# Another order of the opening steps in a packed attention and feed-forward kernel

## The chip, the cores and the metric

The kernel runs on one core of one Trainium2 chip. The metric is the device time of one execution in microseconds (us). Before the change it is 703.89 us, the median of three runs (703.79 to 703.93). The engines are named as the profile names them: PE is the matrix engine (PEld its weight loads), DVE the vector engine, ACT the scalar engine, POOL the GpSimd engine, and SP the engine that issues nearly all DMAs.

## The reference

There are 8 batches of 8 heads, 576 tokens and 64 columns a head. For each head, 32 packing queries `p` attend to the keys and values, and the 576 queries then attend to the 32 packed rows, which serve as keys and values both. The heads are laid side by side (512 columns), and a feed-forward layer of 2048 hidden columns follows.

```python
def sm_attn(qq, kk, vv):
    s = scale * np.matmul(qq, kk.transpose(0, 1, 3, 2))
    a = np.exp(s - np.max(s, axis=-1, keepdims=True))
    a = a / (np.sum(a, axis=-1, keepdims=True) + 1e-09)
    return np.matmul(a, vv)
p_packed = sm_attn(p, k, v)
x = sm_attn(q, p_packed, p_packed)      # tokens x 512
h = x @ w_in                            # 512 x 2048
out = (h * (1.0 / (1.0 + np.exp(-h)))) @ w_out
```

## The kernel before

**The work.** The kernel never builds `x`. It multiplies the packed rows of a batch by `w_in` (a "pack", `pp`, line 250) and the second attention's shares by that product (`h`, line 563), so the hidden values of a batch come from 32 shares a head. A unit is one block of 128 hidden columns of one batch: `h` makes its products, `g` applies the activation (ACT, lines 582 to 588), `l` takes the rounding rest (DVE, line 593), and `o` multiplies by `w_out` and adds up in PSUM (line 603). From the fifth unit on, each product is made of three products of a faster 32-bit type (a high part and a low part of each operand); the first four units (`WHOLE`) use plain float32.

**The weights.** `w_in` and `w_out` arrive as 64-bit numbers in 20 chunks. A chunk is fetched (`wf`, SP, line 191), scaled and rounded on ACT (`ws`, `wr`, lines 197 and 201), bounded, signed and shifted on DVE (`wz`, `wg`, `wt`, lines 205, 209, 216), and joined (`wj`, line 220) on POOL if its number is in `ON_POOL`, else on DVE. Chunks of `w_out` are then split into two parts (`wu` on ACT, line 236; `wl` on DVE, line 240).

**The attention of one batch** is written as steps with a letter each. Those that matter here: `as` scores of the packing queries (PE, line 250, tile `kvq_t`), `ac` their copy to SBUF (ACT, line 276), `am`, `ax` largest value and exponential (DVE 286, ACT 296), `at`, `ay` turning by products with the identity and copying back (PE 315, ACT or DVE 333), `aa` packed rows (PE 348), `an`, `ai`, `aj` scaling, turning and copying them (DVE 358, PE 367, ACT 371, tile `ppT`). Then the second attention, in two halves of the tokens (`.0` and `.1`): `aS` scores (PE 250), `aC` copy (ACT 392), `aB` turning (PE 400), `aM`, `aE` largest and its subtraction (DVE 430, 441), `aX` exponential (ACT 450), `aD`, `aG` sums and shares (DVE 459 to 475), `aU` turning back (PE 420, 423), `aF` copy of the shares (ACT 486), after which `h` may begin.

**The order.** For the first two batches and the weights, nothing is scheduled by a tool: the table `ORDER` (line 54) is read from left to right, and each word is one step; the instructions of a step go to the end of the queues of their engines, in that order, PE, DVE, ACT and SP alike. Each engine works its queue strictly in order, so a waiting instruction holds up all behind it on its engine. The later batches follow a loop with fixed places.

**Filler.** `W` followed by a number is `keep_warm` (line 139): so many products of the identity with itself, whose result nobody reads. One costs two instructions in the trace. The filler's tile comes from `ps_two`, the pool of two PSUM buffers that `as`, `pp` and `h` use as well, so filler may have to wait for a buffer.

**Loads.** Keys, values and queries take turns in a pool of two buffers (`kvq_t`); the queries of batch 0 go to other tiles (`o` and `rest`). Loads and weight chunks share one SP queue.

## Time and profile before

| | |
|---|---|
| median of three runs | 703.89 us |
| the profiled execution's own time | 703.09 us |
| its span, first to last instruction | 701.3 us |
| PE busy | 693.3 us (99%), 5058 matmul instructions |
| DVE, ACT busy | 326.2 us (47%), 331.0 us (47%) |
| POOL busy | 28.7 us (4%) |
| DMA moved | 64.61 MB |

How to read it: the profiled execution spends 1.8 us outside the span of its instructions. PE is busy nearly all the time, so the time can only move where PE waits or does work that isn't needed; the shares of DVE and ACT are averages over the whole span, and in the first 80 us both are far busier than that. In the rows of the time line the first number is the start, the second the length, both in us; `x8` at a row's end is a count of instructions, and brackets name the idle time before them and what ended it.

### The profile page before, as it was taken

The page shows a single profiled execution, that of the slowest core. Times are in us where ns is not written, and L with a number is a line of the kernel's source. Part 1 is how long each engine was busy: PE and PEld are TensorE (multiplying, and loading weights), DVE is VectorE, ACT ScalarE, POOL GpSimd, SP SyncE. Part 2 cuts the span into 40 slices and gives each one's busy share as a digit, 9 for nine tenths or more (in the row PEclk, how much of TensorE's full clock was granted, in tenths as well). Part 3 has the DMA queues.
Part 4 walks back from the last instruction along what each step waited for, and adds up shares of the span by engine and source line. Part 5 has one row for each costly group of instructions (what it writes and reads, how often), then busy time and mean ns, then how long its engine had stood idle before and what let it go on. Part 6 is the DMA issues. An engine that isn't in the chain of part 4 may idle for free.

```text
span 701.3 us, 12059 instructions
## 1 busy us (share of the span) xinstructions
PE 693.3 (99%) x5058; PEld 560.5 (80%) x5058; DVE 326.2 (47%) x482; ACT 331.0 (47%) x614; POOL 28.7 (4%) x19
## 2 busy tenths in 40 slices
PE   8999999999999999999999999999999999999997
PEld 5557788878787888888788888878878788788886
DVE  4999948764534136333532335342372323622111
ACT  4997866637245244451633526452442533433221
POOL 1041022110000000000000000000000000000000
PEclk9999999999999999999999999999999999999999
DMA  9775333634221320313012131123202120010002
GB/s 358 288 304 206 134 121 114 193 141 156 70 81 69 77 104 1 128 33 137 12 61 84 27 107 49 61 72 70 110 0 76 68 36 1 1 60 1 1 1 75
DMA packets 28309, 64.61 MB, mean 92 GB/s; under 512 B 16736, under 2 KB 16736, under 8 KB 23904
## 3 DMA queue, kind: packets, MB, share of 16 engines
q1 hardware_dynamic: 28160, 63.71, 26.2%
q8 instruction: 40, 0.66, 0.4%
q10 hardware_dynamic: 96, 0.13, 0.1%
q14 instruction: 13, 0.11, 0.0%
HBM read 48.76 MB, written 11.53 MB: 86 GB/s over the span
## 4 chain that ended last, share of the span: by engine, by line
PE 97%; ACT 1%; DMA 1%; DVE 1%; issue 0%; ACTq 0%; DVEq 0%
PE ps_acc L603 58%; PE ps_two L563 29%; PE ps_two L250 7%; PE ps_two L348 2%; DMA kvq_t<-in_pkT 1%; PE ps_acc L250 0%; ACT tm L296 0%; PE ps_two L144 0%; ACT tm L392 0%; ACT w_raw L201 0%; ACT win L201 0%; PE ps_two L315 0%; PE ps_two L367 0%; PE ps_acc L315 0%; DVE mx L286 0%
## 5 line engine op out<-in xcount | busy, mean ns | idle before, releaser
L603 PE MATMUL ps_acc<-wo_hi,g_hi 128*128 128x512 f32 x560 | 223.8, 400 | 0.0
L603 PE MATMUL ps_acc<-wo_hi,g_lo 128*128 128x512 f32 x560 | 219.4, 392 | 0.0
L603 PE MATMUL ps_acc<-wo_lo,g_hi 128*128 128x512 f32 x560 | 218.8, 391 | 0.0
L593 DVE TENSOR_TENSOR g_lo<-g,g_hi 128x512 fp32r<-128x512 f32 x124 | 88.9, 717 | 259.5 <-ACT g_hi L584 259.5
L582 ACT ACTIVATE g<-ps_two 128x512 f32<-128x512 f32 x124 | 74.1, 598 | 263.9 <-PE ps_two L563 239.9
L563 PE MATMUL ps_two<-a_lo,pw_hi 128*128 128x288 f32 (+2 forms) x528 | 154.6, 301 | 0.1
L563 PE MATMUL ps_two<-a_hi,pw_hi 128*128 128x288 f32 (+1 forms) x496 | 146.5, 295 | 0.0
L563 PE MATMUL ps_two<-a_hi,pw_lo 128*128 128x288 f32 (+1 forms) x496 | 145.9, 294 | 0.0
L603 PEld LDWEIGHTS ps_acc<-wo_hi,g_hi 128*128 128x128 f32 x560 | 105.1, 188 | 39.3 <-issue 19.9
L603 PEld LDWEIGHTS ps_acc<-wo_hi,g_lo 128*128 128x128 f32 x560 | 105.1, 188 | 24.5 <-DVE g_lo L593 0.4
L603 PEld LDWEIGHTS ps_acc<-wo_lo,g_hi 128*128 128x128 f32 x560 | 105.2, 188 | 18.4
L563 PEld LDWEIGHTS ps_two<-a_lo,pw_hi 128*128 128x128 f32 x528 | 99.1, 188 | 6.2 <-issue 1.4
L563 PEld LDWEIGHTS ps_two<-a_hi,pw_hi 128*128 128x128 f32 x496 | 93.1, 188 | 4.5 <-issue 0.8
L563 PEld LDWEIGHTS ps_two<-a_hi,pw_lo 128*128 128x128 f32 x496 | 93.2, 188 | 0.0
L584 ACT ACTIVATE g_hi<-ps_two 128x512 fp32r<-128x512 f32 x124 | 73.6, 593 | 10.9 <-PE ps_acc L603 10.9
L531 DVE TENSOR_TENSOR pw_lo<-ps_two,pw_hi 128x1024 fp32r<-128x1024 f32 x31 | 36.8, 1219 | 12.8 <-ACT pw_hi L528 12.8
L528 ACT CAST pw_hi<-ps_two 128x1024 fp32r<-128x1024 f32 x31 | 30.2, 1015 | 20.9 <-PE ps_two L250 20.9
L250 PE MATMUL ps_two<-win,ppT 64*32 64x512 f32 (+1 forms) x560 | 32.8, 560 | 0.4 <-POOL win L220 0.4
L586 ACT ACTIVATE rest<-ps_two 128x64 f32<-128x64 f32 x112 | 25.9, 231 | 0.0
L582 ACT ACT_TABLE_LOAD x16 | 20.5, 1283 | 1.5 <-PE ps_two L563 1.0
L250 PEld LDWEIGHTS ps_two<-win,ppT 64*32 64x32 f32 x560 | 7.9, 105 | 14.5 <-issue 11.1
L573 ACT CAST g_hi<-rest 128x512 fp32r<-128x512 f32 x16 | 9.9, 624 | 13.5 <-PE ps_acc L603 13.2
(122 smaller groups left out, 485.0 us busy)
## 6 DMA issues: line engine op xcount, KB each, us to landing
kvq_t<-in_v SPq DMA_DIRECT2D x8, 1280.0 KB, 6.1
kvq_t<-in_pkT SPq DMA_DIRECT2D x7, 1216.0 KB, 6.6
out<-o SPq DMA_DIRECT2D x16, 512.0 KB, 2.8
kvq_t<-in_qT SPq DMA_DIRECT2D x7, 1152.0 KB, 6.5
w_raw<-in_w_in SPq DMA_DIRECT2D x6, 1024.0 KB, 7.5
win<-in_w_out SPq DMA_DIRECT2D x3, 1024.0 KB, 4.5
w_raw<-in_w_out SPq DMA_DIRECT2D x3, 1024.0 KB, 6.2
parts<-o SPq DMA_DIRECT2D x4, 512.0 KB, 5.0
```

The costliest lines, as they stand in the source:

```text
L250: nc.tensor.matmul(bank(par)[NP * i : NP * i + NP], lhs(r, i), rhs(r, i), start=True, stop=True)
L348: nc.tensor.matmul(self.ps[NP * i : NP * i + NP, par * D : par * D + D], e, vs[:n, c, h * D : h * D + D], start=(c == 0), stop=(c == 4),)
L528: nc.scalar.copy(self.hi, self.ps[:, :, : self.nf * P])
L531: nc.vector.tensor_tensor(self.lo, self.ps[:, :, : self.nf * P], self.hi.bitcast(F32), ALU.subtract)
L563: nc.tensor.matmul(bank, p[:, par, cols], a[:, par], start=(n == 0), stop=(n == len(todo) - 1))
L573: nc.scalar.copy(g_hi, g)
L582: nc.scalar.activation(g, ps[..., :MAIN], AF.Silu)
L584: nc.scalar.activation(g_hi, ps[..., :MAIN], AF.Silu)
L586: nc.scalar.activation(to, ps[..., MAIN:HS], AF.Silu)
L593: nc.vector.tensor_tensor(g_lo[:, c], g[:, c], g_hi[:, c].bitcast(F32), ALU.subtract)
L603: nc.tensor.matmul(bank, g[:, rows], w[:, at], start=(first and n == 0), stop=(last and n + 1 == len(todo)))
```

## The change

The change replaces the table `ORDER` by another one with the same steps, except for the filler, and the set `ON_POOL`. The calls of the filler ask for 33 identity products in the old table and for 22 in the new one.

```diff
 ORDER = """
-W7 k0 as0.0 W1 as0.1 am0.0 ax0.0 am0.1 wf0 v0 W4 at0.0 ay0.0 ax0.1 wf1 ws0 at0.1 ay0.1 wr0 wz0 wg0 ar0 W3 aa0 an0 W1
+W7 k0 as0.0 as0.1 am0.0 am0.1 ax0.0 wf0 W4 at0.0 v0 ax0.1 ar0 ay0.0 ws0 wf1 wf2 wr0 wz0 wg0 at0.1 ay0.1 W3 aa0 wt0
...
-ON_POOL = (0, 1, 2, 6, 9, 10, 11, 13, 14, 15, 16, 18, 19)
+ON_POOL = (0, 1, 2, 3, 4, 5, 7, 10, 11, 13, 14, 15, 16, 17, 18, 19)
```

Chunks 3, 4, 5, 7 and 17 are now joined on POOL, and chunks 6 and 9 on DVE. Further down, the units' steps stand in another order among the weights' steps, and the last two loads of the table (keys and values of batch 3) have changed places.

What stands on PE between the turning of the packed rows of batch 0 (L367) and the first output product (L603), before. Line 250 appears four times: with `o` and `rest` (the two halves of the second scores), with `win` (a pack), and with `kvq_t` (the scores of batch 1).

```order
L250 MATMUL ps_acc<-o,ppT 32x256 x8
L144 MATMUL ps_two<-ident 128x128 x2
L400 MATMUL ps_acc<-ident,tm 128x128 x4
L250 MATMUL ps_acc<-rest,ppT 32x320 x8
L144 MATMUL ps_two<-ident 128x128 x11
L400 MATMUL ps_acc<-ident,tm 128x128 x6
L250 MATMUL ps_two<-win,ppT 32x128 x8
L420 MATMUL ps_acc<-ident,tm 128x128 x4
L250 MATMUL ps_two<-win,ppT 32x128 x8
L144 MATMUL ps_two<-ident 128x128
L563 MATMUL ps_two<-a_lo,pw_hi 128x256 x4
L144 MATMUL ps_two<-ident 128x128 x2
```

The same place now:

```order
L250 MATMUL ps_acc<-o,ppT 32x256 x8
L250 MATMUL ps_acc<-rest,ppT 32x320 x8
L400 MATMUL ps_acc<-ident,tm 128x128 x10
L250 MATMUL ps_two<-win,ppT 32x128 x8
L144 MATMUL ps_two<-ident 128x128
L250 MATMUL ps_two<-win,ppT 32x128 x8
L250 MATMUL ps_two<-kvq_t 32x288 x8
L420 MATMUL ps_acc<-ident,tm 128x128 x4
L250 MATMUL ps_two<-kvq_t 32x288 x8
L144 MATMUL ps_two<-ident 128x128 x2
L563 MATMUL ps_two<-a_lo,pw_hi 128x256 x4
```

The scores of batch 1 (`kvq_t`), which stood behind the first unit's products (L563), now stand ahead of them, one half on each side of the first turning back (L420), and the filler of 2 and of 11 products is gone from between the steps of the second attention.

What stands on ACT there, from the first weight steps to the copy of the second scores, as the difference from the old order to the new. L197 and L201 are weight steps, L371 copies `ppT`, L392 copies the second scores.

```order
+L197 ACTIVATE w_raw<-w_raw 128x512
 L201 ACTIVATE w_raw<-w_raw 128x512
 L197 ACTIVATE w_raw<-w_raw 128x512
+L371 COPY ppT<-ps_acc 128x128
 L201 ACTIVATE w_raw<-w_raw 128x512
-L371 COPY ppT<-ps_acc 128x128
 L392 COPY tm<-ps_acc 128x2x256
+L392 COPY tm<-ps_acc 128x2x320
+L236 CAST wo_hi<-o 128x512
```

The copy of `ppT`, without which the second scores can't begin, now stands behind weight steps of chunk 2 and chunk 1; in the old order they were those of chunks 0 and 1.

What stands on SP at the start, again as the difference; `in_pkT` holds packing queries and keys, and the one with 128x2432 is that of batch 1.

```order
 L191 DMA w_raw<-in_w_out 128x512
+L191 DMA w_raw<-in_w_in 128x512
 L159 DMA o<-in_qT 128x1024
 L159 DMA rest<-in_qT 128x1280
-L191 DMA w_raw<-in_w_in 128x512
 L191 DMA w_raw<-in_w_out 128x512
 L191 DMA win<-in_w_in 128x512
+L150 DMA kvq_t<-in_pkT 128x2432
 L191 DMA win<-in_w_out 128x512
-L150 DMA kvq_t<-in_pkT 128x2432
```

A weight chunk has moved ahead of the queries, and the keys of batch 1 have moved ahead of a weight chunk.

## The prediction

> **What bounds the kernel now.** I read the page first, then PE's waits, then a table of the first 60 us by stretches, then the time lines of PE and ACT in the first 50 us.

> ```profile
> span 701.3 us, 12059 instructions
> PE 693.3 (99%) x5058; PEld 560.5 (80%) x5058; DVE 326.2 (47%) x482; ACT 331.0 (47%) x614; POOL 28.7 (4%) x19
> ```

> PE is busy for 693.3 of 701.3 us, so all idle time of PE together is 8 us. The waits of PE that the trace can name are five, all in the opening; the two longest:

> ```profile
> PE ps_two L144 <- POOL ident masks.py:199: 1.4, 1, 1.4
> PE ps_acc L315 <- ACT tm L296: 0.9, 1, 0.9
> ```

> By stretches (columns: PE, PEld, DVE, ACT, POOL busy, granted clock, DMA share, GB/s):

> ```profile
> 15.00:20.00 5.00, 4.82 (x48) 3.75 (x49) 4.65 (x10) 3.33 (x6) 1.64 (x2) 1.00 1.02 411
> 30.00:40.00 10.00, 10.00 (x46) 5.54 (x45) 9.45 (x14) 9.44 (x19) 2.19 (x1) 1.00 0.64 246
> 40.00:50.00 10.00, 10.00 (x140) 5.54 (x138) 9.86 (x14) 9.82 (x18) 3.53 (x2) 1.00 0.68 269
> ```

> From 30 us on PE has no idle time, and neither order has filler there; that work is the same in both. So the change can move the end only by when the row of full work begins, and by stalls that it newly makes behind that point. Until then PE waits or runs filler, and the DMA queues run full (share 1.02, 411 GB/s).

> ```profile
> 1.36 3.36 PE L144 MATMUL ps_two<-ident 128*128 128x128 f32 x14 [1.36 <-POOL ident masks.py:199]
> ...
> 14.27 0.67 PE L250 MATMUL ps_acc<-o,ppT 64*32 64x256 f32 x16
> ...
> 15.74 0.66 PE L400 MATMUL ps_acc<-ident,tm 128*128 128x128 f32 x4 [0.15 <-ACT tm L392]
> ...
> 17.02 2.72 PE L144 MATMUL ps_two<-ident 128*128 128x128 f32 x22
> 19.77 0.88 PE L400 MATMUL ps_acc<-ident,tm 128*128 128x128 f32 x6
> ...
> 21.14 0.63 PE L420 MATMUL ps_acc<-ident,tm 128*128 128x128 f32 x4
> ...
> 26.39 1.20 PE L250 MATMUL ps_two<-kvq_t 64*32 64x288 f32 x32
> 27.53 0.44 PE L420 MATMUL ps_acc<-ident,tm 128*128 128x128 f32 x2
> ...
> 28.67 1.98 PE L603 MATMUL ps_acc<-o,g_hi 128*128 128x512 f32 x4
> ...
> 43.69 1.03 PE L563 MATMUL ps_two<-a_lo,pw_hi 128*128 128x256 f32 x4
> 44.56 1.88 PE L603 MATMUL ps_acc<-o,g_hi 128*128 128x512 f32 x4
> ```

> The mark is the first output product, at 28.67 us. Up to it PE does the same work in both orders, filler apart (scores, packs 0 and 1, both turnings back, batch 1's scores, the first eight product rows), and behind it PE is full. Where it lands after the change is the main term.

> **The filler.** Eleven of 33 identity products go. Between 17.02 and 19.77, 22 rows, that is 11 products, take 2.75 us: 0.25 us each. At face value the change gains 11 x 0.25 = 2.75 us. But filler counts only where the step behind it could have begun earlier, so I follow what the first unit waits for.

> **The keys of batch 1.** Their scores now stand ahead of the first unit's products, so PE waits for their load.

> ```profile
> 3.27 0.49 SPq L159 DMA_DIRECT2D o<-in_qT  x1
> 3.80 0.44 SPq L159 DMA_DIRECT2D rest<-in_qT  x1
> ...
> 6.18 0.33 SPq L191 DMA_DIRECT2D win<-in_w_in  x1
> ```
> ```profile
> kvq_t<-in_pkT SPq DMA_DIRECT2D x7, 1216.0 KB, 6.6
> ...
> win<-in_w_in SPq DMA_DIRECT2D x2, 512.0 KB, 13.5
> ...
> rest<-in_qT SPq DMA_DIRECT2D x1, 640.0 KB, 11.0
> ...
> o<-in_qT SPq DMA_DIRECT2D x1, 512.0 KB, 9.9
> ```

> The load is behind ten transfers now, the same ten that end with `win<-in_w_in` before. That one landed at 6.18 + 13.5 = 19.7 (13.5 is a median of two). 1216 KB are 1.245 MB; at 411 GB/s they take 3.0 us: the keys land at 22.7. In the old order one more chunk of 512 KB (1.3 us) stood ahead, so about 24.0, and they weren't read before 26.39. It could be sooner. The second half of the queries landed at 3.80 + 11.0 = 14.8, and the weight chunk behind it, by the ACT row below, at 17.15: 2.35 us for what takes 1.3. If that delay of about 1.0 us doesn't come again, the keys land at 21.7.

> **From the keys to the first output product.**

> ```profile
> 11.44 0.69 ACT L201 ACTIVATE w_raw<-w_raw 128x512 int32<-128x512 uint32 x1
> 12.03 0.71 ACT L197 ACTIVATE w_raw<-w_raw 128x512 f32<-128x512 f32 x1
> ...
> 13.96 0.27 ACT L371 COPY ppT<-ps_acc 128x128 f32<-128x128 f32 x1 [0.66 <-PE ps_acc L367]
> ...
> 17.15 0.69 ACT L197 ACTIVATE w_raw<-w_raw 128x512 f32<-128x512 f32 x1 [1.47 <-DMA w_raw<-in_w_in]
> ...
> 22.15 0.58 ACT L486 COPY a_lo<-ps_acc 128x512 f32<-128x512 f32 x1
> ...
> 27.21 1.18 ACT L276 COPY tm<-ps_two 128x576 f32<-128x576 f32 x2 [0.20 <-PE ps_two L250]
> ```

> First half of batch 1's scores: both halves took 27.53 - 26.39 = 1.14 us, one takes 0.57, so 22.75 to 23.3. Turning back (L420, 0.63): to 23.95. ACT copies the shares (L486, 0.6 to the next): to 24.6; then the two copies of batch 1's scores, which ACT now has ahead of the activation (L276, 1.18): to 25.8. The second half of the scores lies beside that on PE. The scores hold both buffers of `ps_two`; the filler of 2 takes the one that the first copy frees (25.2) and ends by 25.7, hidden behind the second copy, and the products of the first unit get the other at 25.8. Eight rows of them: 2 x (44.56 - 43.69) = 1.74, to 27.55. Second turning back, by the old rows 28.67 - 27.53 = 1.14: to 28.7. The first output product starts at 28.7, against 28.67. The 2.75 us of filler are traded for a wait of some 2.3 us on a load and for two copies ahead of the first unit.

> **The other chain to the same place.** PE's order behind the keys needs the first half's shares too, and those come later than before. The third weight chunk takes the place of the first half of the queries: it lands at 3.27 + 9.9 = 13.2. ACT scales it (L197) and, strictly in order, holds `ppT` behind it: three weight steps of 0.6 (11.44 to 12.03) end at 15.0, the copy (0.27) at 15.3, and the second scores, which began at 14.27, begin at 15.3. Queued behind that on ACT is nothing that PE needs sooner. The second half of the queries now lands where that chunk landed, 17.1, or 16.0 without the delay. Its scores (0.67) end at 17.8 or 16.8, and only then come the first turnings (L400), at 15.74 before. From there to the turning back it took 21.14 - 15.74 = 5.4 us. DVE has the other half's largest value and subtraction (0.95 and 0.96) between, and three weight steps (0.43, 0.43, 0.63) less:

> ```profile
> 17.87 0.43 DVE L205 TENSOR_SCALAR w_raw<-w_raw 128x512 f32<-128x512 f32 x1
> 18.33 0.43 DVE L216 TENSOR_SCALAR win<-w_raw 128x512 int32<-128x512 int32 x1
> ...
> 19.77 0.63 DVE L209 SCALAR_TENSOR_TENSOR w_raw<-w_raw 128x512 int32<-128x512 int32 x1
> ...
> 20.91 0.95 DVE L430 TENSOR_REDUCE on_tokens<-ps_acc 128x24 f32<-128x768 f32 x1
> 21.96 0.96 DVE L441 TENSOR_TENSOR tm<-ps_acc,on_tokens 128x768 f32<-128x768 f32 x1
> ```

> So 5.8 us: shares at 22.6 to 23.6, against 23.3 by the keys. If both the keys and the queries come early, the mark falls by 0.7, to 28.0; if the queries come late, it rises by 0.3. That chain is why an early load can't give much.

> **Behind the mark.** DVE and ACT have 0.2 to 0.6 us to spare in 10 us there (9.45, 9.86 and 9.44, 9.82 above), so a step that is late can show on PE. Of DVE's joins, five in the first 50 us become three. POOL gets more, and a POOL join can hold DVE up:

> ```profile
> 43.70 2.77 POOL L220 TENSOR_TENSOR win<-win,w_raw 128x1024 int32<-128x1024 int32 x1 [5.78 <-DVE w_raw L209]
> ```
> ```profile
> 44.14 2.89 DVE L205 TENSOR_SCALAR win<-win 128x1024 f32<-128x1024 f32 x1
> ```

> The DVE step (L205) begun under that join lasted until 0.56 us behind its end, instead of some 0.7; it cost 2.2 us, and PE still did not wait. [...] I put new stalls at 0.2 us, with ends of 0 (as before) and 1.0 (half of one such hold-up reaches PE). The loads of batch 3, which change places at the table's end, have slack: the last of the two was issued at 190.25 and takes 6.6, and the keys are read at 210.25.

> ```profile
> 190.25 1.09 SPq L169 DMA_DIRECT2D kvq_t<-in_v  x1
> ```
> ```profile
> 210.25 1.20 PE L250 MATMUL ps_two<-kvq_t 64*32 64x288 f32 x32
> ```

> **The sum.** 0.0 (the mark) + 0.2 (stalls) on the profiled execution's 703.1 (span 701.3 and 1.8 around it) gives 703.3. The median of the runs shown, 703.89, is 0.8 above that execution, so I forecast 704.1. About 0.2%, or 1.4 us, is what a measurement can tell from no change; the forecast's own range, -0.9 to +1.3, is inside it: 703.0 to 705.2.

> **Rivals.** *The matrix clock falls (slower).* The first 14 filler rows, on a cold start, took 3.36 us, 0.24 a row; the 22 later ones took 0.125. The granted clock reads 1.00 in every stretch, so only the durations show it. The new order leaves PE without work for some 2.3 us ahead of the keys, behind small products; the old one never did, its longest wait behind the start is 0.9. If PE turns cold there, its work on the path from 22.75, 0.57 + 0.63 + 1.74 + 1.14 = 4.1 us, doubles for as long as it stays so; over half of it, about 2 us: 706.1. It decides if the rows of L563 near 26 us are twice as long. [...] Chance 0.12.

> *DVE falls behind under POOL's joins (slower).* If one hold-up like the 2.2 us above reaches PE whole, 706.1; it shows only where DVE's slack is used up. Against it: DVE has fewer joins. Chance 0.13.

> *The filler is the price (faster).* If the loads and the shares come early enough for the full 2.75 us, 701.3. Against it stand the full DMA queues. Chance 0.08.

> *It doesn't do what it says*: three filler products still stand between the packs and the first unit; they are in the sum.

> **The numbers.** Forecast 0.67, slower 0.25, faster 0.08. Range 702.8 to 706.2: it takes in the forecast's bounds and the two slower rivals' prices, and leaves out the faster one and hold-ups that add up. Same 0.67, as the forecast's bounds lie within 1.4 us.

> **What would show it.** Right: PE's first wait for the keys of batch 1 of some 2 us, ending near 22.7; first output product near 28.7; no idle PE behind 30 us. Wrong: that product before 27.3 or behind 30; L144 or L563 rows twice as long near 26 us; waits of PE for DVE between 30 and 80 us that sum to over a microsecond.

## The result, and the profile after

The changed kernel takes 707.25 us (median of four runs, 706.76 to 708.17), the kernel before 703.84 in the same session: a ratio of 1.0050, 95% interval 1.0034 to 1.0066. It is slower by 3.4 us, outside the forecast range. The profiled execution of the changed kernel is the longest of its four runs, 708.17, and the one profiled before, 703.09, lies under all the runs shown before; so the two profiles are further apart (5.1 us) than the medians. Lines of the changed kernel's page:

```profile
span 706.4 us, 12020 instructions
PE 694.8 (98%) x5036; PEld 559.2 (79%) x5036; DVE 327.0 (46%) x479; ACT 328.2 (46%) x612; POOL 32.9 (5%) x22
```

PE's work has hardly changed (694.8 against 693.3 us, with 11 filler products less); the span is 5.1 us longer. So the time is in waits and in work at a lower clock. PE's waits, the largest first, with the one at the very start left out:

```profile
PE ps_acc L250 <- DMA rest<-in_qT: 1.5, 1, 1.5
...
PE ps_acc L420 <- DVE tm L475: 0.8, 1, 0.8
...
PE ps_two L250 <- ACT rest L588: 0.7, 1, 0.7
PE ps_two L250 <- DMA kvq_t<-in_pkT: 0.5, 1, 0.5
```

The first, second and fourth are new waits of the opening. The time line of PE from the second scores to the mark, the first output product:

```profile
17.35 1.11 PE L250 MATMUL ps_acc<-rest,ppT 64*32 64x320 f32 x16 [1.50 <-DMA rest<-in_qT]
18.39 2.41 PE L400 MATMUL ps_acc<-ident,tm 128*128 128x128 f32 x10
...
22.81 0.72 PE L250 MATMUL ps_two<-kvq_t 64*32 64x288 f32 x16 [0.49 <-DMA kvq_t<-in_pkT]
24.38 1.07 PE L420 MATMUL ps_acc<-ident,tm 128*128 128x128 f32 x4 [0.85 <-DVE tm L475]
25.38 1.21 PE L250 MATMUL ps_two<-kvq_t 64*32 64x288 f32 x16
...
27.68 2.00 PE L563 MATMUL ps_two<-a_lo,pw_hi 128*128 128x256 f32 x8
...
30.59 1.98 PE L603 MATMUL ps_acc<-o,g_hi 128*128 128x512 f32 x4
```

The mark is at 30.59, against 28.67 before. The same two halves of batch 1's scores took 0.72 and 1.21 us: between them the clock changed. The table by stretches shows it; its edges are 3.41 us apart, and from 17.64 on they are put where the granted clock changes. In a row, the numbers behind the edges are the length, the busy time of PE, PEld, DVE, ACT and POOL, each with a count in brackets, the granted clock, the DMA share and GB/s:

```profile
14.23:17.64 3.41, 1.62 (x31) 0.84 (x37) 2.59 (x6) 2.11 (x5) 0.75 (x1) 1.00 1.03 408
17.64:21.05 3.41, 3.41 (x42) 2.08 (x26) 1.48 (x3) 1.21 (x2) 2.18 (x2) 0.50 1.00 417
21.05:24.47 3.42, 1.94 (x51) 0.82 (x36) 3.35 (x7) 3.42 (x7) 0.00 (x0) 1.00 1.04 418
24.47:27.88 3.41, 3.34 (x25) 2.02 (x26) 3.27 (x7) 3.06 (x6) 0.00 (x0) 0.50 1.02 419
```

PE was busy for 1.62 us of the first stretch and then ran at half clock for 3.41 us; busy for 1.94 us of the third, and again at half clock for 3.41 us.

The rest of the loss is far behind the mark. The packed rows of batch 2 (line 348) run from

```profile
L348 PE MATMUL ps_two<-kvq_t,tm x80: 216/219/243, 144.1 to 145.7; 128*32 128x64 f32 x64, 64*32 64x64 f32 x16
```

before, and now from

```profile
L348 PE MATMUL ps_two<-kvq_t,tm x80: 216/219/243, 149.2 to 150.8; 128*32 128x64 f32 x64, 64*32 64x64 f32 x16
```

That is 5.1 us later, 1.9 of it from the mark. Matched product by product, PE is 2.1 us behind the old kernel at 119 us, 5.0 at 150, and 5.1 at the end: nearly all of the other 3.2 is lost between 120 and 150. Rows of several engines of the changed kernel, in order of time:

```profile
120.78 6.15 POOL L220 TENSOR_TENSOR win<-win,w_raw 128x1024 int32<-128x1024 int32 x2 [9.18 <-ACT w_raw L201]
121.70 2.94 DVE L593 TENSOR_TENSOR g_lo<-g,g_hi 128x512 fp32r<-128x512 f32 x1
...
124.74 1.28 ACT L582 ACT_TABLE_LOAD   x1 [1.76 <-DVE g_lo L593]
...
127.16 0.69 DVE L593 TENSOR_TENSOR g_lo<-g,g_hi 128x512 fp32r<-128x512 f32 x1 [2.51 <-ACT g_hi L584]
...
129.14 1.09 PE L250 MATMUL ps_two<-win,ppT 64*32 64x512 f32 x16 [0.71 <-ACT rest L588]
...
131.84 1.12 ACT L197 ACTIVATE w_raw<-w_raw 128x1024 f32<-128x1024 f32 x1 [1.85 <-DMA w_raw<-in_w_out]
...
135.18 0.39 PE L563 MATMUL ps_two<-a_hi,pw_hi 128*128 128x256 f32 x1 [0.40 <-DVE pw_lo L531]
```

POOL joins chunks 16 and 17 back to back. Unit 17's rounding rest (L593), 0.69 us when alone, takes 2.94 beside the first of them, ACT waits for it with the next unit, and PE at last for a pack's buffer. Then ACT waits 1.85 us for the load of chunk 18, ahead of a pack's copy that PE needs. The kernel before has no wait of PE in this stretch. (PE's idle time in it, 1.63 us in the changed kernel, is less than the 2.9 us that it falls behind: products of line 603 that follow each other directly start 0.23 us apart and are listed with 0.39, so idle time leaves out a part of each wait.)

### The profile page after: what moved, and what is told of

It is laid out like the page before. It is cut to its first block, busy times and chain, and to the rows that moved or that the text cites. A ratio compares the mean times of both kernels' runs of the same rounds, so it can differ in the third digit from the quotient of the medians.

```text
span 706.4 us, 12020 instructions
## 1 busy us (share of the span) xinstructions
PE 694.8 (98%) x5036; PEld 559.2 (79%) x5036; DVE 327.0 (46%) x479; ACT 328.2 (46%) x612; POOL 32.9 (5%) x22
## 3 DMA queue, kind: packets, MB, share of 16 engines
q1 hardware_dynamic: 28160, 63.71, 25.8%
## 4 chain that ended last, share of the span: by engine, by line
PE 91%; DMA 3%; issue 2%; DVE 1%; ACT 1%; POOL 0%; SPq 0%; ACTq 0%; POOLq 0%
PE ps_acc L603 55%; PE ps_two L563 27%; PE ps_two L250 6%; DMA rest<-in_qT 2%; PE ps_two L348 2%; DMA w_raw<-in_w_out 1%; POOL win L220 0%; PE ps_acc L420 0%; DVE on_tokens L430 0%; SPq L191 0%; PE ps_two L315 0%; DVE wo_lo L240 0%; DVE w_raw L209 0%; PE ps_two L144 0%; ACT w_raw L197 0%
## 5 line engine op out<-in xcount | busy, mean ns | idle before, releaser
L603 PE MATMUL ps_acc<-wo_hi,g_hi 128*128 128x512 f32 x560 | 223.8, 400 | 0.0
L603 PE MATMUL ps_acc<-wo_hi,g_lo 128*128 128x512 f32 x560 | 219.5, 392 | 0.1
L603 PE MATMUL ps_acc<-wo_lo,g_hi 128*128 128x512 f32 x560 | 218.8, 391 | 0.2 <-DVE wo_lo L240 0.2
L593 DVE TENSOR_TENSOR g_lo<-g,g_hi 128x512 fp32r<-128x512 f32 x124 | 88.3, 712 | 268.3 <-ACT g_hi L584 266.9
L563 PE MATMUL ps_two<-a_lo,pw_hi 128*128 128x288 f32 (+2 forms) x528 | 154.5, 301 | 0.0
L563 PE MATMUL ps_two<-a_hi,pw_hi 128*128 128x288 f32 (+1 forms) x496 | 147.0, 296 | 0.5 <-DVE pw_lo L531 0.4
L563 PE MATMUL ps_two<-a_hi,pw_lo 128*128 128x288 f32 (+1 forms) x496 | 145.9, 294 | 0.0
L603 PEld LDWEIGHTS ps_acc<-wo_hi,g_hi 128*128 128x128 f32 x560 | 105.1, 188 | 39.1 <-issue 19.9
L603 PEld LDWEIGHTS ps_acc<-wo_hi,g_lo 128*128 128x128 f32 x560 | 105.1, 188 | 24.7 <-DVE g_lo L593 0.5
L603 PEld LDWEIGHTS ps_acc<-wo_lo,g_hi 128*128 128x128 f32 x560 | 105.2, 188 | 19.1 <-DVE wo_lo L240 0.5
L563 PEld LDWEIGHTS ps_two<-a_lo,pw_hi 128*128 128x128 f32 x528 | 99.4, 189 | 6.1 <-issue 1.4
L563 PEld LDWEIGHTS ps_two<-a_hi,pw_hi 128*128 128x128 f32 x496 | 93.1, 188 | 5.5 <-DVE pw_lo L531 0.9
L563 PEld LDWEIGHTS ps_two<-a_hi,pw_lo 128*128 128x128 f32 x496 | 93.1, 188 | 0.0
L528 ACT CAST pw_hi<-ps_two 128x1024 fp32r<-128x1024 f32 x31 | 30.4, 1016 | 18.3 <-PE ps_two L250 18.2
L250 PE MATMUL ps_two<-win,ppT 64*32 64x512 f32 (+1 forms) x560 | 33.2, 563 | 1.0 <-ACT rest L588 0.7
L250 PEld LDWEIGHTS ps_two<-win,ppT 64*32 64x32 f32 x560 | 7.9, 106 | 16.2 <-issue 11.1
L384 DVE STREAM_TRANSPOSE tm<-ps_two 128x288 f32<-128x288 f32 x28 | 11.1, 452 | 9.6 <-PE ps_two L250 9.6
## 6 DMA issues: line engine op xcount, KB each, us to landing
kvq_t<-in_pkT SPq DMA_DIRECT2D x7, 1216.0 KB, 6.8
out<-o SPq DMA_DIRECT2D x16, 512.0 KB, 2.8
parts<-o SPq DMA_DIRECT2D x4, 512.0 KB, 2.8
```

Source lines behind the costliest of these rows:

```text
L250: nc.tensor.matmul(bank(par)[NP * i : NP * i + NP], lhs(r, i), rhs(r, i), start=True, stop=True)
L384: nc.vector.transpose(t[:, par * HS : par * HS + HS], self.half[hf][:, par, :HS])
L528: nc.scalar.copy(self.hi, self.ps[:, :, : self.nf * P])
L563: nc.tensor.matmul(bank, p[:, par, cols], a[:, par], start=(n == 0), stop=(n == len(todo) - 1))
L593: nc.vector.tensor_tensor(g_lo[:, c], g[:, c], g_hi[:, c].bitcast(F32), ALU.subtract)
L603: nc.tensor.matmul(bank, g[:, rows], w[:, at], start=(first and n == 0), stop=(last and n + 1 == len(todo)))
```

## The experiments

My theory after this: two losses that have little to do with each other, the opening (late queries and half clock) and the stretch from 120 to 150 us (joins on POOL, a late load). The rivals: the later loss follows from the late opening; the loads alone set the opening, and the clock is a side show; the set of joins alone costs the time.

All runs in one table. The ratio is to the kernel before in the same session, with its 95% interval; 0.001 is 0.7 us. The mark is the start of the first output product in the profiled execution (the same step has another line number where a kernel has more lines).

| kernel | median us | ratio | mark us |
|---|---|---|---|
| the changed kernel | 707.25 | 1.0050 (1.0034 to 1.0066) | 30.59 |
| before_then_after | 706.36 | 1.0032 (1.0020 to 1.0044) | 28.72 |
| after_then_before | 705.07 | 1.0010 (0.9995 to 1.0025) | 29.90 |
| before_cut | 704.57 | 1.0001 (0.9987 to 1.0014) | 29.54 |
| fill_waits | 707.67 | 1.0050 (1.0032 to 1.0067) | 29.79 |
| q_first | 707.98 | 1.0053 (1.0038 to 1.0068) | 30.94 |
| turn_first | 707.56 | 1.0048 (1.0029 to 1.0067) | 30.85 |
| first_half | 707.38 | 1.0051 (1.0037 to 1.0064) | 29.66 |
| keys_behind | 707.26 | 1.0049 (1.0035 to 1.0062) | 29.59 |
| lower_first | 706.21 | 1.0027 (1.0016 to 1.0037) | 29.40 |
| join17_dve | 707.27 | 1.0041 (1.0026 to 1.0056) | 29.72 |
| later_part | 706.03 | 1.0031 (1.0020 to 1.0041) | 31.12 |
| mended | 706.18 | 1.0034 (1.0021 to 1.0047) | 29.95 |
| all_mended | 706.02 | 1.0030 (1.0019 to 1.0042) | 29.78 |
| before_new_pool | 704.49 | 1.0004 (0.9995 to 1.0014) | 29.16 |
| join16_alone | 705.61 | 1.0026 (1.0016 to 1.0037) | 29.68 |
| whole | 705.39 | 1.0019 (1.0010 to 1.0028) | 30.10 |
| scores_back | 705.96 | 1.0030 (1.0019 to 1.0042) | 30.01 |
| before_less_2 | 703.33 | 0.9988 (0.9980 to 0.9997) | 28.45 |

### Two losses or one?

Both tables are cut at step `o0.0`, the first output product, and put together crosswise: the steps up to it from one, the steps that are left from the other, in that one's order.

> The kernel before up to the first output product (step o0.0), and from there the changed kernel's order and set of joins on POOL. If the stalls between 120 and 150 us belong to the later part of the new order: first output product at 28.7, PE's waits between 120 and 150 us of 1.0 to 3.0, and 704.9 to 706.9. If they come of the late opening: no such waits, and 703.7 to 704.1.

> The changed kernel up to the first output product (step o0.0), and from there the order and the set of joins of the kernel before. If the two losses add up, opening 1.9 and later part some 1.5: first output product at 30.4 to 30.8, no wait of PE between 120 and 150 us, and 705.4 to 706.2. If the later part's loss follows from the late opening: waits of 1 us or more stay between 120 and 150, and 706.8 to 707.6.

The old opening with the new later part: mark 28.72, and PE busy for only 28.80 us of the stretch from 120 to 150; ratio 1.0032, about 2.3 us. The new opening with the old later part: mark 29.90, all 30.00 us busy from 120 to 150; ratio 1.0010, about 0.7 us, not clear of zero. Together some 3.0 of the 3.5 us. Each also has a wait at the seam, 0.44 and 0.71 us near 34 us, that neither parent has, so these two runs don't give each loss to the tenth. But there are two losses, and the later one, the larger, doesn't follow from the opening.

### The later part

First, one word moved, the rounding rest of unit 17 ahead of the step that lets the join begin:

```diff
-... wr17 wt17 wt16 wj16 ax2.0 wg17 l17 h19 ...
+... wr17 l17 wt17 wt16 wj16 ax2.0 wg17 h19 ...
```

> The changed kernel with one word moved: the rounding rest of unit 17 (l17, L593 on DVE) ahead of the shifts of chunks 17 and 16 and so ahead of the join on POOL that follows them. Hold-up theory (that step lasted 2.94 us at 121.70 because the join ran, ACT waited for it with the next unit, and PE with a pack): it takes 0.7 us, PE's wait of 0.7 us at 129.14 and the smaller ones at 124.7 and 127.3 go, and the time falls by 0.9 to 1.5. Rival (the wait comes of the ACT table loads and the place of the two packs): the wait at 129 stays over 0.5 us and the time within 0.4.

Rows of POOL, DVE and PE in that kernel:

```profile
120.17 5.67 POOL L220 TENSOR_TENSOR win<-win,w_raw 128x1024 int32<-128x1024 int32 x2 [9.80 <-issue]
...
124.19 2.21 DVE L593 TENSOR_TENSOR g_lo<-g,g_hi 128x512 fp32r<-128x512 f32 x1 [3.01 <-ACT g_hi L584]
...
127.68 1.09 PE L250 MATMUL ps_two<-win,ppT 64*32 64x512 f32 x16 [0.69 <-ACT rest L588]
```

Unit 17's rest is free (0.68 us, at 118.15), and the next unit's is now held, for 2.21 us, by the second join. The wait of 0.7 stayed, so half of the expectation failed. So the second join goes too:

```diff
-... wg17 h19 ... g18 l18 wj17 pp8 ...
+... wg17 wj17 h19 ... g18 l18 pp8 ...
-ON_POOL = (0, 1, 2, 3, 4, 5, 7, 10, 11, 13, 14, 15, 16, 17, 18, 19)
+ON_POOL = (0, 1, 2, 3, 4, 5, 7, 10, 11, 13, 14, 15, 16, 18, 19)
```

> The changed kernel with the rounding rest of unit 17 first, as in the run before, and chunk 17's join back on DVE, right behind that chunk's sign step, where DVE had 3.0 us without work (121.2 to 124.2). The join of chunk 16 stays on POOL and nothing follows it there. Hold-up theory, second form (in the run before the join of chunk 17 on POOL held the next unit's rounding rest for 2.21 us): that step takes 0.7 us, PE's waits at 125.9 (0.27) and 127.7 (0.69) go, and the time is 0.8 to 1.2 under the run before, 705.0 to 705.4. Rival (table loads and the place of the packs): the wait of about 0.7 at 127 to 129 stays, 706.0 to 706.4.

The waits at 126 and 128 went, and PE waited later instead. ACT and PE in that kernel:

```profile
130.82 1.15 ACT L197 ACTIVATE w_raw<-w_raw 128x1024 f32<-128x1024 f32 x1 [2.71 <-DMA w_raw<-in_w_out]
...
134.18 0.39 PE L563 MATMUL ps_two<-a_hi,pw_hi 128*128 128x256 f32 x1 [1.73 <-DVE pw_lo L531]
```

The price that was expected to go (about 1 us) came back as 1.73 at the next place, and the time, forecast at 705.0 to 705.4, was 707.27: ACT's step for chunk 18 waits for its load, ahead of pack 9's copy. That pair was swapped:

```diff
-... pp9 pl8 ws18 wz18 ay2 pu9 pl9 o18 ...
+... pp9 pl8 pu9 pl9 ws18 wz18 ay2 o18 ...
```

> The changed kernel with three moves in the later part: unit 17's rounding rest first and chunk 17's join on DVE (as in join17_dve), and the copy and rounding rest of pack 9 ahead of chunk 18's first steps, which wait for that chunk's load. ACT order theory: PE's wait of 1.73 at 134 us goes as well, what is left between 120 and 150 us is under 0.5, and the time is 1.5 to 2.6 under the changed kernel's, 704.8 to 705.6. Rival (the pack's rest is late for DVE's own work): a wait of over 1 us stays at 134, 706 or more.

The wait at 134 went, and waits of 0.52 and 0.39 for ACT came at 138.7 and 140.9, behind ACT's steps for chunks 18 and 19, which waited 1.75 and 1.98 us for their loads; the time, 706.03, stayed above the 704.8 to 705.6 that were expected. So each cure passed the wait on. What the later waits share is the load of chunk 18. Its issue on SP, before:

```profile
117.97 0.33 SPq L191 DMA_DIRECT2D w_raw<-in_w_out  x1
118.39 1.59 SPq L652 DMA_DIRECT2D parts<-o  x2
```

and in the changed kernel:

```profile
119.48 0.33 SPq L652 DMA_DIRECT2D parts<-o  x1
124.12 3.17 SPq L191 DMA_DIRECT2D w_raw<-in_w_out  x2
```

Chunk 18 takes the buffer of chunk 16, which is free when chunk 16 is joined. The old order joins it on POOL at 115.50, in 2.45 us, the new one at 120.78, in 3.31 us, some five microseconds later; and the load of chunk 18 is issued six microseconds later than before, at 124.12 instead of 117.97, each time 0.02 us behind the join's end. A part of these six is SP's own order: the load now stands behind another load (values of batch 2) and both stores of `parts`, and those alone would hold it until 119.8. The rest is the buffer. The last edit of this row moves, in the changed kernel, only that shift and join:

```diff
-... ws17 l15 o14 ... wr17 wt17 wt16 wj16 ax2.0 ...
+... ws17 l15 wt16 wj16 o14 ... wr17 wt17 ax2.0 ...
```

> The changed kernel with one step of chunk 16, its shift and so its join on POOL, moved ahead by some 7 us (behind the rounding rest of unit 15, about 112 us), where DVE has 2.8 us without work; nothing else. Root theory (that join was late, ran back to back with chunk 17's, held a rounding rest of DVE and kept the buffer for chunk 18's load until 124): that load is issued at about 119, ACT's weight step for it no longer waits at 130, the waits of PE between 120 and 150 us fall from about 1.6 to under 0.8, and the time is 0.7 to 1.8 under the changed kernel's, 705.4 to 706.5. Rival (the set of joins alone, chunk 17 on POOL, makes the 0.7 us wait): the wait of 0.7 at 128 to 129 stays and only the one near 135 goes, under 0.5 gained.

POOL and SP in that kernel:

```profile
112.67 2.43 POOL L220 TENSOR_TENSOR win<-win,w_raw 128x1024 int32<-128x1024 int32 x1 [1.97 <-DVE win L216]
118.99 4.63 SPq L191 DMA_DIRECT2D w_raw<-in_w_out  x2
120.44 2.82 POOL L220 TENSOR_TENSOR win<-win,w_raw 128x1024 int32<-128x1024 int32 x1 [5.34 <-DVE w_raw L209]
```

The stretch from 120 to 150 us (length, then PE, PEld, DVE, ACT, POOL, clock, DMA), first in the changed kernel, then in this one:

```profile
120.00:150.00 30.00, 28.37 (x203) 21.78 (x201) 21.47 (x24) 19.58 (x33) 9.94 (x4) 1.00 0.60 188
120.00:150.00 30.00, 29.73 (x259) 22.98 (x258) 19.15 (x25) 19.84 (x33) 6.61 (x3) 1.00 0.54 180
```

POOL has 5.34 us without work between the joins, the load is issued at 118.99, directly behind the store of `parts`, and PE is idle for 0.27 us, against 1.63. The ratio fell from 1.0050 to 1.0026, 1.7 us. One step's place explains most of the later loss. It mends the held rounding rests and the late load at once, so this run doesn't say what each is worth. In this kernel and in the run whole, chunk 16's shifted numbers land on the place of chunk 14 before that chunk's rounding rest is taken, so that rest, and with it the output, is computed from other numbers, by the same instructions: the early place isn't to be had as it stands, and the two kernels are here for their times alone.

The set of joins alone, in the old order:

> The kernel before with the new set of joins on POOL alone. If the set by itself costs time (more steps of DVE behind a join): waits of PE of 0.7 to 2 us in sum behind 30 us, 704.6 to 705.8. If it is harmless in an order made for other joins: within 0.3 of the kernel before, 703.7 to 704.3.

A wait of 0.69 for ACT at 127.10, where the old kernel has none, and a ratio of 1.0004 (0.9995 to 1.0014) that can't be told from 1. By itself, in the old order, the set costs at most 1.0 us, so it is not the whole cause.

### The filler and the clock

The kernel before without `W11`, and the changed kernel with eleven products in its waits:

> The kernel before without the filler of 11 ahead of the turning of the second half, the rest as it was. Filler at face value: the first output product starts 2.75 us sooner, at 25.9, and the time is 701.1. Data theory (something else holds that place anyway): it starts at 28.5 to 28.8, 703.6 to 704.0. Clock theory: the stretch from 17.1 to about 19.8 becomes idle, the granted clock falls to 0.5 for a stretch behind it, and the product starts at 29.2 to 30.0; 704.4 to 705.2.

> The changed kernel with eleven identity products put back where its PE waits: six ahead of the second half of the second scores (behind the 1.50 us wait for the queries), two ahead of batch 1's scores and three ahead of the first turning back, each written into the bank that the next product overwrites, so that no buffer changes. Clock theory (PE's clock halved because it had too little work in the stretches before): the granted clock reads 1.00 from 15 to 30 us, the ten turnings (L400) take 1.5 us instead of 2.41, the first output product starts at 29.0 to 29.4 instead of 30.59, and the time falls by 1.2 to 1.6, to about 705.7 to 706.1. Load theory (the queries' landing at 17.35 sets it, the clock is a side show): the product starts at 30.4 to 30.9 and the time stays at 707.2.

Stretches, and PE's rows, in before_cut:

```profile
15.22:18.63 3.41, 1.58 (x22) 0.63 (x21) 2.70 (x6) 1.49 (x4) 1.29 (x1) 1.00 1.02 406
18.63:22.04 3.41, 2.21 (x23) 1.50 (x24) 3.21 (x7) 2.86 (x6) 1.28 (x1) 0.50 1.02 424
```
```profile
19.83 1.54 PE L400 MATMUL ps_acc<-ident,tm 128*128 128x128 f32 x6 [2.87 <-ACT tm L392]
```

Without its filler the wait of 2.87 us stands open, the turning begins at 19.83 as it did with it (19.77), and the clock halves. The mark is 0.87 us later, the measured time the same within its interval. So, as forecast, the eleven products don't cost their face value: that is 2.75 us, and the interval leaves at most 0.9. With filler in its waits the changed kernel's clock reads 1.00 from 15 to 30 us, and the mark is at 29.79; the time is not better. Six of the kernels have the very same opening, and show how much is chance, in one profile each:

| kernel | half clock from 15 to 30 us | mark us |
|---|---|---|
| the changed kernel | twice 3.4 us | 30.59 |
| later_part | twice | 31.12 |
| lower_first | once | 29.40 |
| join16_alone | once | 29.68 |
| join17_dve | once | 29.72 |
| after_then_before | once | 29.90 |

The two with a second stretch at half clock have their marks 1.2 us later in the mean (30.86 against 29.68). One such stretch doesn't show in the mark: fill_waits and the five other kernels with filler in their waits (mended, keys_behind, all_mended, whole and scores_back) read 1.00 throughout, and their marks are 29.59 to 30.10 (all but the first differ in order, too). So up to 1.2 of the 1.9 us in the changed kernel's profile go with the second stretch at half clock, and 0.9 to 1.4 us stay at full clock. The changed kernel's own four runs spread over 1.4 us, the old kernel's over 0.2 in that session; but in a later session single runs of the old kernel reached 707 and 708, so that the clock makes this spread is not shown.

### The order of the opening

Each cure takes out one more place where a step of the first half waits behind another. In q_first the queries are fetched ahead of the third weight chunk; in turn_first the first half is turned ahead of the second half's scores; first_half, besides that, puts the first half's sums and shares on DVE ahead of the second half's largest value, and its exponential on ACT ahead of a copy of weights; keys_behind adds filler to first_half and lets the turning back pass batch 1's scores. mended is turn_first with filler, with the later part of join17_dve. In the rows below, the first two are turn_first's, the last two what keys_behind has besides.

```diff
-... aC0.0 wj1 aS0.1 wj0 aC0.1 aB0.0 aB0.1 ...
+... aC0.0 wj1 aB0.0 aS0.1 wj0 aC0.1 aB0.1 ...
-... aM0.1 wr3 aD0.0 pu1 ws3 aE0.1 aX0.1 ws4 aG0.0 ... k1 as1.0 aD0.1 aG0.1 aU0.0 aF0.0 ac1.0 ...
+... aD0.0 aG0.0 aM0.1 wr3 pu1 ws3 aE0.1 aX0.1 ws4 ... k1 aU0.0 aF0.0 as1.0 aD0.1 aG0.1 ac1.0 ...
```

> The changed kernel with the queries of batch 0 fetched ahead of the third weight chunk again, and that chunk's steps on ACT and DVE moved behind the copies of the second scores. Load theory: the second half of the queries lands 1.3 to 1.5 us sooner, at about 15.9, PE's wait for it goes, and the first output product starts at 28.7 to 29.3; about 705.4 to 705.9. Clock theory: the wait goes as well, but there is still little work on PE between 15 and 18 us; if the granted clock falls to 0.5 there as before, the product starts no sooner than 29.8 (706.4 or more).

> The changed kernel with one word moved: the turning of the first half of the second scores (aB0.0) ahead of the second half's scores (aS0.1), as in the old table. PE's queue theory (the first half's chain on DVE starts late only because its turning stands behind products that wait for a load): the four turnings run at about 16.7, inside the wait for the queries, DVE's first largest value starts at about 17.4 instead of 19.54, the first turning back begins at 22.0 to 22.8 instead of 24.38, and the first output product at 28.6 to 29.6, by how much of it still runs at half clock; the time falls by 1.0 to 2.0. Load theory (the queries and the keys set it): the product stays at 30.3 to 30.9 and the time within 0.4.

> The same, and the opening with both cures at once: the first half's turning ahead of the second half's scores, and eleven identity products (2, 2, 3, 2 and 2) written into the banks of the steps that wait. Clock and queue theory together: the clock reads 1.00 up to 30 us, the first turning back follows the first half of batch 1's scores at 23.4 to 23.9 (the keys land at about 22.8), the first output product starts at 28.7 to 29.2, and with no waits behind 60 us the time is 704.0 to 704.6. If the opening is bound by the loads whatever the clock and the order do: first output product at 29.6 to 30.2, 705.0 to 705.6.

> The changed kernel with the first half's steps ahead of the second half's again: its turning on PE ahead of the second half's scores, its sums and shares on DVE ahead of the second half's largest value, its exponential on ACT ahead of a copy of weights. No filler. DVE order theory: the sums (L459) follow the exponential at about 20 instead of 21.7 to 22.1, the first turning back comes right behind the first half of batch 1's scores, at 23.4 to 23.9 (later if that part runs at half clock), and the first output product at 28.4 to 29.4; the time is 0.8 to 1.8 under the changed kernel's. Load theory (all waits for the second half's queries or the keys anyway): first output product at 29.6 to 30.6 as in the variants so far.

> The same, with eleven identity products in the waits as in the run mended, and the first turning back and its copy ahead of batch 1's scores, so that they don't wait for the keys. If order and clock are the cause: the clock reads 1.00 up to 30 us, the first turning back begins at 21.3 to 22.2, the scores with the keys at about 22.9, and the first output product at 27.4 to 28.4, ahead of the kernel before (28.67); the time is 2.2 to 3.0 under the changed kernel's, 704.6 to 705.2, with the later part's waits still in it. If the loads bound it: first output product at 29.2 or later.

None of them moved the time: 1.0048 to 1.0053 for the four that have the changed kernel's later part. In q_first the second half's scores ran at 15.02, and PE then waited 2.7 us for the pack of the chunk that had given way. DVE in turn_first:

```profile
18.62 0.69 DVE L441 TENSOR_TENSOR tm<-ps_acc,on_tokens 128x512 f32<-128x512 f32 x1
21.22 0.96 DVE L430 TENSOR_REDUCE on_tokens<-ps_acc 128x24 f32<-128x768 f32 x1 [1.91 <-PE ps_acc L400]
22.09 0.67 DVE L459 TENSOR_REDUCE on_tokens<-tm 128x16 f32<-128x512 f32 x1
```

The first half's subtraction is done at 19.3, and its sums (L459) wait behind the second half's largest value, which waits for the queries. With that mended, ACT in keys_behind (L458 is the exponential of the second half, L494 the copy of the first shares, L281 the copies of batch 1's scores):

```profile
23.68 0.85 ACT L458 ACTIVATE tm<-tm 128x768 f32<-128x768 f32 x1 [0.77 <-DVE tm L449]
24.43 0.65 ACT L201 ACTIVATE win<-win 128x512 f32<-128x512 f32 x1
24.98 0.57 ACT L494 COPY a_lo<-ps_acc 128x512 f32<-128x512 f32 x1
25.44 1.18 ACT L281 COPY tm<-ps_two 128x576 f32<-128x576 f32 x2
```

The first shares were turned back by 22.9 (PE's row at 22.34, 0.60 long) and were copied at 24.98. So the new table lets the second half of the tokens pass the first on PE, DVE and ACT one after the other, and a cure on one engine meets the next. With all of them taken out, and at last with batch 1's scores behind the first unit again:

> The opening of keys_behind and the later part of later_part together. If the causes found are all there is: first output product at 27.4 to 28.4, no wait of over 0.3 us behind it, and 702.9 to 703.8, that is 0.1 to 1.0 under the kernel before. If something else in the new order costs time: 704.2 or more.

> The changed kernel with all causes found so far taken out. Opening: the first half's turning, sums, shares, turning back and copy ahead of the second half's steps on PE, DVE and ACT, the weight steps of chunks 3 and 4 behind the copies of batch 1's scores, and eleven identity products in the waits. Later part: chunk 16's join early, chunk 17's on DVE, unit 17's and pack 9's steps ahead of the weights'. If the causes are complete: the copy of the first shares (L486 in the old numbering) starts at about 22.5 to 23.2, the first output product at 27.6 to 28.6, no wait over 0.3 us behind it, and 702.8 to 703.8, as fast as the kernel before or up to 1.0 faster. If the loads (keys at 23, queries at 17.5) bound the opening: first output product at 29 or later, 704.2 to 705.

> The opening of the run whole with batch 1's scores and their copies behind the first unit's products again, and the later part of later_part (chunk 16's join in the changed kernel's place). Order theory (the scores ahead of the unit are the last cost): the first shares are copied at about 23.0 to 23.7, the first unit's products start at 23.9 to 24.8 instead of 26.7 to 27.2, the scores follow without a wait for the keys, and the first output product starts at 28.4 to 29.2; with the later part's waits of about 1 us still in it the time is 704.4 to 705.4. Load theory (whatever the order, the queries' landing some 1 us later than before sets it): first output product at 29.6 or later, 705.5 or more.

Marks of 29.78, 30.10 and 30.01: the expectations failed, and the marks are those that the load theory gave for whole and scores_back (whole's time, 705.39, is a little above its 704.2 to 705). PE in scores_back:

```profile
16.05 0.67 PE L254 MATMUL ps_acc<-o,ppT 64*32 64x256 f32 x16 [1.08 <-ACT ppT L375]
...
24.48 1.99 PE L570 MATMUL ps_two<-a_lo,pw_hi 128*128 128x256 f32 x8 [0.23 <-ACT a_lo L493]
```

The second scores begin at 16.05, against 14.27 before, because the copy of `ppT` stands behind the steps of the third chunk, whose load came at 14.05 (at 13.17 in the changed kernel's profile, where the scores begin at 15.18). That first link no cure but q_first took out, and q_first paid for it at the other end. That the opening is bound by which of the third chunk and the queries comes first fits the marks of all these kernels; no run showed it alone, and what makes up the last microsecond of the opening stays open.

### A faster kernel

The kernel before without the filler of 2 ahead of batch 1's scores:

```diff
-... ws6 W2 as1.0 ...
+... ws6 as1.0 ...
```

> The kernel before without the filler of 2 ahead of batch 1's scores (25.62 to 26.33, behind a wait of 0.43 us for a buffer). Face value: these two products delay what follows, the first output product starts 0.7 us sooner, at about 27.9, and the time falls by 0.4 to 0.7, to 703.2 to 703.5. Clock theory: the stretch from 23 to 27 us is full enough without them (over 0.8 of it busy), the clock reads 1.00, the same gain. Chain theory (ACT or DVE set what follows): the product starts sooner, but waits of PE between 28 and 40 us take it back, and the time is 703.8 to 704.0.

```profile
26.17 1.21 PE L250 MATMUL ps_two<-kvq_t 64*32 64x288 f32 x32 [0.44 <-ACT g_hi L582]
...
28.45 1.98 PE L603 MATMUL ps_acc<-o,g_hi 128*128 128x512 f32 x4
```

The scores follow the wait for a buffer directly. The ratio is 0.9988 (0.9980 to 0.9997), about 0.8 us faster than the kernel before (0.2 to 1.4), and so faster than both; the face value of those two products, 0.71 us, lies inside that. The profiles don't show it as clearly: the mark is 0.22 us sooner and not 0.7, because in this execution the wait for the buffer ended at 26.17 instead of 25.62, and its time, 703.57, is above the 703.09 of the one profiled before. The gain rests on the runs, twelve of this kernel against 29.

## Why the prediction was wrong

**The bound** held: between 30 and 120 us PE is idle for under 0.2 us, and the time moved by the mark and by new stalls behind it. **The filler** brought nothing, as forecast: before_cut gains nothing by as many products, the `W11` alone.

**The keys of batch 1** landed at 22.8, forecast 22.7. But PE waited 0.49 us for them and not 2.3: it came late itself.

**The other chain** is the first step that failed: "So 5.8 us: shares at 22.6 to 23.6". Its start was right: the third chunk came at 13.17 (forecast 13.2), the second scores began at 15.18 (15.3). But the turning back began at 24.38. The queries landed at 17.35, by the late end of the range; their scores took 1.04 us to the next step, mostly at half clock, and not 0.67 (which is the first half's row; the second half's took 0.70 before); and the 5.8 us were 6.0. I let the keys set the mark and took this chain as a check. I also counted only the length of the second half's two steps on DVE (0.95 and 0.96), not that these wait for the late queries and hold the first half's sums behind them.

**From the turning back to the mark** I had 5.4 us (23.3 to 28.7), and 6.2 came, the half clock again. **The clock rival** had a chance of 0.12, because I judged it by PE's longest single wait: 2.3 us was forecast, and I took that as too short, by an estimate of mine that no run shows. The traces show another measure, how much of a stretch of 3.41 us is busy. In the one ahead of the first half clock PE was busy for 1.62 us, and its longest wait was 1.50 us.

**The stalls behind the mark** are the larger miss: 0.2 us forecast, ends 0 and 1.0; by before_then_after about 2.3, its wait of 0.44 at the seam included. The step that failed is "I put new stalls at 0.2 us, with ends of 0 (as before) and 1.0": its rows end at 50 us, and I followed no moved step behind that except the loads of batch 3. The hold-up that I priced at 2.2 us did come, at 121.70 with 2.94, and behind it a load that I hadn't followed: its buffer is freed by a join that moved, and it moved in SP's list too, behind two stores and another load.

**The rivals** were taken one at a time. The two slower ones both happened, in part; their prices on top of the forecast, 2.0 each, would have given 708.1, against 707.25. The new set of joins, which I counted against the change, did not cost measurably by itself. The range has a small slip as well: by its own terms (the mark -0.7 to +0.3, the stalls 0 to 1.0, on 703.9) the forecast's lower bound is 703.2 and not 703.0.

## What to carry to other kernels

In a hand-written order a step's place matters on every queue at once: for each step that moves, ask what it frees (a buffer, and through it a load), and what stands behind it on its engine, to the end of the program and not only near the change. Where each cure moves a wait on to the next place, look for what the waits share, which here was a join that came five microseconds late and the load behind it, and move that. Filler can be free inside a wait and cost time outside one; measure it by taking out one piece at a time, since here the runs gained nothing without one piece (the 11) and some 0.8 us without another (the 2).

## What was not expected of the hardware

```profile
15.72:19.13 3.41, 1.91 (x37) 0.90 (x24) 2.30 (x5) 1.75 (x4) 2.14 (x2) 1.00 1.05 426
19.13:22.54 3.41, 1.83 (x40) 1.04 (x38) 3.31 (x7) 2.60 (x7) 0.80 (x1) 1.00 0.98 404
22.54:25.95 3.41, 3.12 (x36) 1.20 (x36) 3.27 (x8) 2.60 (x5) 0.00 (x0) 0.50 1.06 428
...
22.70:26.12 3.42, 1.82 (x39) 0.98 (x37) 3.28 (x7) 2.65 (x6) 0.00 (x0) 1.00 1.06 425
26.12:29.53 3.41, 3.40 (x18) 2.71 (x18) 3.38 (x5) 3.33 (x5) 1.42 (x1) 1.00 1.00 420
```

In the first kernel 1.91 us were enough and 1.83 were not; in the second 1.82 were enough, and in the changed kernel 1.94 were not. In the first 50 us of these profiles the clock always fell behind stretches with less than 1.8 us (just over half), never behind those with more than 1.94, and went either way between the two. And one opening gave one or two such stretches in six profiles, with the mark moving by 1.7 us, so one profile of a kernel with stretches near 1.8 to 1.94 us doesn't show its spread.
